# A decode attention kernel: TensorE's code walked twice, and the wait for the stores in a section of its own

## The chip, the cores and the metric

The kernel runs on one core of a Trainium2 chip. The metric is the device time of one execution in microseconds (us). Three executions of the kernel before took 826.02, 824.43 and 824.61 us; their median is 824.61 us.

## What is computed

Two attention layers, A and B, each for a single new token (batch 1, one query row), with 32 heads of 128 columns, caches of 16384 positions and a model width of 512. B looks at the last 4096 positions alone. The rest is the same for both:

```
q = (x @ wq) split into 32 heads
scores = q . k * 128 ** -0.5          # per head, over the positions
p = softmax(scores)
o = p @ v                             # per head
out = o (32 heads x 128, in a row) @ wo    # 512 columns
result = concatenate(out of A, out of B)   # 1 x 1 x 1024, bf16
```

A reads all of k and v, B a quarter of them. One query row means that each byte of k and v is used once.

## The kernel before, in words

**Units.** The work is cut into 20 units, numbered in the order B0, A0 to A15, B1, B2, B3. A unit of A holds two heads, one of B four heads; either one has 8 MB of k and 8 MB of v. k has two buffers in SBUF, v has one.

**Engines.** SyncE (SP) issues the loads of k, v and the weights. VectorE (DVE) multiplies k by q (L365), adds the products up in a tree (L377, L384) and takes maxima (L393, L416). TensorE (PE) turns the per-lane maxima into a row (L399, `unit_max`), spreads the maxima (L421, `max_all`), sums the exponentials (L472, `soft_sum`), multiplies p by v (L492, `pv`) and picks each head's columns (L514, `columns`). ScalarE (ACT) does the exponentials and the copies. DVE works on the scores of one unit while PE and ACT finish the one before it.

**Stream.** `_Stream` keeps a list of operations for each engine and works out which semaphores each has to wait on. `finish` (L140) writes them out, engine by engine. Operations of the A units are marked as one loop (`st.loop`), and `_emit_loop` (L123) writes the body once, inside a hardware loop (`Fori`, L132). So PE's code is, in this order: the projections and unit B0; the loop that serves A0 to A15; then, written out, B1 and B2, the output projection of A, and B3 with the output projection of B. All of it is passed once, from top to bottom.

**The end.** The last unit, B3, is split up to follow its loads. Its v comes in two halves: VL0 in a k buffer and VL1 in the v buffer (L678). For each half, `pv_columns` (L527) issues 128 matmuls at L532. `permute_o` (L544) then rearranges the heads' results (L548, L549, L553, L560). wo of B is loaded in five pieces of 16, 8, 4, 3 and 1 rows (L601, L683), issued right behind VL1. `project_out_columns` (L575) issues four matmuls for each row, so 64, 32, 16, 12 and 4 at L583, and the first of each piece waits for that piece. DVE adds up (L591), PE transposes (L595), DVE copies to a row (L597), and SP stores it (L598, semaphore outB). The store of A's row (outA) has been issued earlier by ACT (L573). Last, an empty operation on SP waits for both stores (L697).

**The section.** Everything in the stream stands in one critical section (L698). In the built program the section's exit is a round on semaphores: SP signals, every engine answers, SP collects the answers and signals once more. The program's own last barriers (L725) come after it.

Of the kernel before, what the change touches and what calls it, by code (L numbers as in the profile page):

```python
# [12 lines left out]
ACT = mybir.ActivationFunctionType  # L13
# [3 lines left out]
HQ, DH = 32, 128  # L17
# [7 lines left out]
class _Op:  # L25
    def __init__(self, eng, idx, emit, dma, tok, loop):
        self.eng, self.idx, self.emit, self.dma, self.tok, self.loop = eng, idx, emit, dma, tok, loop
        self.known, self.waits, self.takes, self.sem, self.count = None, [], [], None, None


class _Stream:
# [6 lines left out]

    def __init__(self, nc):
        self.nc = nc
        self.eng = {"PE": nc.tensor, "DVE": nc.vector, "ACT": nc.scalar, "SP": nc.sync, "POOL": nc.gpsimd}
        self.ops = {e: [] for e in self.eng}
        self.known = {e: {} for e in self.eng}
        self.writer, self.readers = {}, {}
        self.sems, self.tokens, self.counts, self.taken = {}, {}, {}, set()
        self.loop = {}

    def sem(self, name):  # L50
        if name not in self.sems:
            self.sems[name] = self.nc.alloc_semaphore(name)
        return self.sems[name]

    def _mark(self, op):
# [8 lines left out]
        k, v = self._mark(op)  # L64
        return known.get(k, -1) >= v

    def op(self, eng, emit, r=(), w=(), dma=None, tok=None, takes=()):
        assert all(k in self.writer or "." in k for k in r), r
        known = self.known[eng]
        op = _Op(eng, len(self.ops[eng]), emit, dma, tok, self.loop.get(eng))  # L70
        for t in takes:
            src = self.tokens[t].pop(0)
            self.taken.add(t)
            op.takes.append((t, 16 if src.dma is not None else 1))
            self._learn(known, src)
        need = [(self.writer[k], True) for k in [*r, *w] if k in self.writer]
        need += [(x, False) for k in w for x in self.readers.get(k, [])]
        need = [x for x, hard in need if x.eng != eng or x.dma is not None or (hard and eng != "PE")]

        def can_wait(x):  # L80
            if x.sem in self.taken:
                return False
            if op.loop is not None:
                return x.eng == eng and x.loop == op.loop and x.tok is None
            return x.loop is None or x.tok is not None or x.eng == "PE"

        for src in sorted(need, key=lambda x: (not can_wait(x), x.dma is None, -x.idx)):
            if self._knows(known, src):
                continue
            assert can_wait(src), (eng, op.idx, op.loop, src.eng, src.idx, src.sem, src.loop)  # L90
            op.waits.append((src.sem, src.count))
            self._learn(known, src)
        op.known = dict(known)
        if op.loop is not None and eng != "PE" and dma is None and tok is None:
            op.sem = f"{eng}{op.loop[0]}"
            base = sum(1 for o in self.ops[eng] if o.loop == op.loop and o.sem == op.sem)
            op.count = base + 1
        else:
            op.sem = tok or dma or eng
            self.counts[op.sem] = op.count = self.counts.get(op.sem, 0) + (16 if dma is not None else 1)  # L100
        self.tokens.setdefault(op.sem, []).append(op)
        self.ops[eng].append(op)
        for k in r:
            self.readers.setdefault(k, []).append(op)
        for k in w:
            self.writer[k], self.readers[k] = op, []
        return op
# [29 lines left out]
                name, n = own[0].sem, own[-1].count  # L137
                self.eng[eng].wait_ge(self.sem(name), n).then_inc(self.sem(name), -n)

    def finish(self):  # L140
        for eng in ("SP", "ACT", "POOL", "DVE", "PE"):
            ops, i = self.ops[eng], 0
            while i < len(ops):
                if ops[i].loop is None:
                    self._emit(eng, ops[i])
                    i += 1
                    continue
                j = i
                while j < len(ops) and ops[j].loop is not None and ops[j].loop[0] == ops[i].loop[0]:
                    j += 1  # L150
                self._emit_loop(eng, ops[i:j])
                i = j


@with_exitstack
def kernel(
# [14 lines left out]
    nc = tc.nc  # L171
# [46 lines left out]
    A, B = _Side(), _Side()  # L218
# [11 lines left out]

    NA, NB = HQ // 2, HQ // 8
    NT = NA + NB
    st = _Stream(nc)
    V, T_, S, G, L = nc.vector, nc.tensor, nc.scalar, nc.gpsimd, nc.sync

    def by_head(s, ap):
# [247 lines left out]
    def pv(un):  # L484
        s, n, g = un.s, un.n // 4, un.s.groups

        def mms():
            for i in range(n):
                for v in range(s.parts):
                    r0 = 32 * (v * g + i % g)  # L490
                    l = v * n + i
                    x = T_.matmul(  # L492
                        s.o[r0 : r0 + un.rows, :],
                        lhsT=un.pm[:, l, :, :].rearrange("p a b -> p (a b)"),
                        rhs=VS[:, 4 * l : 4 * l + 4, :],
                        start=(i < g), stop=(i >= n - g),
                    )
            return x

        st.op("PE", mms, r=["v0", "v1"] + [f"pm0.{j}" for j in range(4)], w=["o" + s.n], takes=["V0"] if s is A else ["V0", "V1"], tok="pv")  # L500

    def evict(un):
        s = un.s
# [23 lines left out]
    def pv_columns(un, v, V_t, vk, ps, pk, pmk, takes):  # L527
        s = un.s

        def mms():  # L530
            for l in range(un.n):
                x = T_.matmul(  # L532
                    ps[:, 0 : s.nh], lhsT=V_t[:, l, :], rhs=un.pm[:, (v * un.n + l) // 4, :, l % 4],
                    start=(l == 0), stop=(l == un.n - 1),
                )
            return x

        st.op("PE", mms, r=[vk] + [f"{pmk}.{j}" for j in range(4)], w=[pk], takes=takes)
        st.op("DVE", lambda: V.tensor_tensor(  # L539
            out=s.O[:, un.col(v) : un.col(v) + s.nh], in0=ps[:, 0 : s.nh],  # L540
            in1=r_t[:, v * s.nh : (v + 1) * s.nh], op=ALU.mult,
        ), r=[pk, "r"], w=[f"O{s.n}.{un.col(v)}"])
# [19 lines left out]
    def project_out_rows(s, key):  # L562
        ps = oc_t[0:1, 0:DN]

        def mms():
            for r in range(HQ):
                x = T_.matmul(ps, lhsT=s.Op[:, r : r + 1], rhs=s.wo_t[:, r, :], start=(r == 0), stop=(r == HQ - 1))
            return x

        st.op("PE", mms, r=["Op" + s.n, key], w=["oc"])  # L570
        row = osb[0:1, 0 : DN // 2].bitcast(BF16)
        st.op("ACT", lambda: S.copy(row, ps), r=["oc"], w=["osb"])
        st.op("ACT", lambda: S.dma_start(out=out[0, 0:1, 0:DN], in_=row), r=["osb"], w=["outA"], dma="outA")  # L573

    def project_out_columns(s, key, pieces):  # L575
        nf, npc = DN // P, len(pieces)
        ps = OC2[:, 0 : npc * nf].rearrange("p (k c) -> p k c", k=npc)
        r0 = 0
        for k, n in enumerate(pieces):
            def mms(k=k, n=n, r0=r0):  # L580
                for c in range(nf):
                    for r in range(r0, r0 + n):
                        x = T_.matmul(  # L583
                            ps[:, k, c : c + 1], lhsT=s.wo_t[:, r, c * P : (c + 1) * P], rhs=s.Op[:, r : r + 1],
                            start=(r == r0), stop=(r == r0 + n - 1),
                        )
                return x

            st.op("PE", mms, r=["Op" + s.n, f"{key}.{k}"], w=["oc2"])
            r0 += n  # L590
        st.op("DVE", lambda: V.tensor_reduce(  # L591
            out=cols[:, :], in_=ps.rearrange("p k c -> p c k"), axis=AX.X, op=ALU.add
        ), r=["oc2"], w=["cols"])
        pr = TP[0][0:nf, 0:P]
        st.op("PE", lambda: T_.transpose(pr, cols[:, :], identf[:, :]), r=["cols", "identf"], w=["tp0"])  # L595
        rows = p_t[0:nf, 0:P]
        st.op("DVE", lambda: V.tensor_copy(rows, pr), r=["tp0"], w=["p.0", "p.1"])  # L597
        st.op("SP", lambda: L.dma_start(out=out[0, 0, DN : 2 * DN].rearrange("(c f) -> c f", c=nf), in_=rows),  # L598
              r=["p.0"], w=["outB"], dma="outB")
# [4 lines left out]
    for s in (B, A):  # L604
        s.x_row = flat(KS[1][0:1, :, :])[:, x0 : x0 + D]
        for a, b in ((0, D // 4), (D // 4, D // 2), (D // 2, D)):
            st.op("ACT", lambda s=s, a=a, b=b: S.dma_start(out=s.x_row[:, a:b], in_=s.x[0, 0:1, a:b]),
                  w=["x" + s.n], dma=f"x{s.n}{a}")
# [15 lines left out]
    for s in (B, A):  # L624
# [9 lines left out]
          w=["k10", "k11", "xA", "xB"] + [f"k10.{j}" for j in range(4)], dma="K10")  # L634
# [59 lines left out]
    pv_columns(un, 1, VS[:, 0:CH, :], "v0", OC2, "oc2", "pm1", ["pm1"])  # L694
    permute_o(B)
    project_out_columns(B, "wo", wo_pieces)
    st.op("SP", lambda: None, r=["outA", "outB"], w=["end"])  # L697
    with tc.tile_critical(no_gpsimd_drain=True):  # L698
        st.finish()


# [28 lines left out]
```

## Time and profile before

| | |
|---|---|
| median of three executions | 824.61 us |
| the profiled execution's own time | 825.75 us |
| its span in the profile | 823.9 us |
| VectorE busy | 762.6 us (93%) |
| TensorE matmuls busy | 197.0 us (24%), 1985 matmuls |
| ScalarE busy | 60.0 us (7%) |
| moved by DMA | 352.45 MB, 428 GB/s over the span |

The span runs from the first to the last recorded instruction; 1.85 us of the profiled execution's own time lie outside it. All moments below are microseconds from the start of the span. An entry such as "PE oc L583 x112" is a group of 112 instructions of TensorE of line 583 that write the tile oc. The view of the DMA queues counts a queue of kind "instruction" apart from the data queues: what engines load of their own code. Code before the loop, the loop and the code behind it are told apart by the unit that they serve.

### The profile page before, as it was taken

To read this page: it belongs to the slowest core of one execution; us is meant where nothing else is said; L and a number is where in the kernel's file an instruction comes from. 1 tells how busy PE (TensorE), PEld (TensorE's weight loads), DVE (VectorE), ACT (ScalarE), POOL (GpSimd) and SP (SyncE) were. 2 spreads that over 40 slices of the span, in tenths; PEclk is the share of its full clock that TensorE was granted. 3 is DMA by queue.
4 is the path that set the end of the run, shared out by engine and by line. 5 is a ranking of instruction groups with operands and counts; after the bars stand their busy time and mean duration, and the time that the engine had idled before them with its cause. 6 is when DMAs were issued, how large, how long until landed. Compare 5 with 4: busy or idle time off the path is not lost. (4 is left out here: it accounts for less than half of the span.)

```text
span 823.9 us, 5048 instructions
## 1 busy us (share of the span) xinstructions
PE 197.0 (24%) x1985; PEld 98.7 (12%) x1985; DVE 762.6 (93%) x353; ACT 60.0 (7%) x168; POOL 0.7 (0%) x6
## 2 busy tenths in 40 slices
PE   0710313213030403030312213030303030213265
PEld 0200101101010101010101101010101010101125
DVE  2399999999999999999999999999999999999980
ACT  0100100001010101010000000010101000010110
POOL 0000000000000000000000000000000000000000
PEclk9965555555565556565556565565655565655585
DMA  9999999999999999999999999999999999999996
GB/s 382 433 433 433 456 411 449 417 449 420 449 423 442 433 433 436 430 439 426 445 420 449 420 452 414 452 417 449 417 449 417 449 412 433 433 433 432 433 429 268
DMA packets 8095, 352.45 MB, mean 428 GB/s; under 512 B 915, under 2 KB 1046, under 8 KB 1302
## 3 DMA queue, kind: packets, MB, share of 16 engines
q1 hardware_dynamic: 8072, 352.33, 99.1%
q8 instruction: 6, 0.10, 0.0%
q14 instruction: 3, 0.02, 0.0%
q10 hardware_dynamic: 14, 0.00, 0.0%
HBM read 352.32 MB, written 0.00 MB: 428 GB/s over the span
## 5 line engine op out<-in xcount | busy, mean ns | idle before, releaser
L377 DVE TENSOR_TENSOR k<-k 128x8192 bf16<-128x8192 bf16 (+3 forms) x160 | 344.9, 2156 | 4.8
L365 DVE TENSOR_TENSOR k<-k,qA 128x16384 bf16<-128x16384 bf16 x32 | 277.9, 8684 | 1.7 <-DVEq L116 1.7
L492 PE MATMUL oA<-v,pm 128*8 128x512 bf16 x1024 | 91.2, 534 | 28.5 <-PEq L116 28.5
L399 PE MATMUL sm<-identf,m 128*1 128x128 f32 x24 | 8.1, 370 | 322.6 <-PEq L116 322.6
L365 DVE TENSOR_TENSOR k<-k,qB 128x16384 bf16<-128x16384 bf16 x8 | 69.5, 8684 | 6.6 <-ACT qB L354 6.6
L421 PE MATMUL sm<-one_f,Mr 1*128 1x1 f32 x48 | 12.3, 335 | 168.4 <-PEq L116 168.4
L384 DVE TENSOR_REDUCE sc<-k 128x128 f32<-128x1024 bf16 x40 | 48.8, 1220 | 0.7
L399 PEld LDWEIGHTS sm<-identf,m 128*1 128x1 f32 x24 | 1.7, 80 | 324.6 <-issue 324.6
L440 ACT ACTIVATE bias<-sm 128x1 f32<-128x1 f32 (+1 forms) x20 | 3.4, 171 | 506.4 <-ACTq L116 506.4
L492 PEld LDWEIGHTS oA<-v,pm 128*8 128x8 bf16 x1024 | 30.4, 112 | 82.3 <-issue 74.6
L421 PEld LDWEIGHTS sm<-one_f,Mr 1*128 1x128 f32 x48 | 11.2, 299 | 174.8 <-issue 174.8
L504 ACT ACTIVATE osb<-oA,r 128x512 f32<-128x512 f32 x16 | 11.0, 687 | 133.5 <-ACTq L116 133.5
L514 PE MATMUL oc<-selA,osb 128*128 128x2 f32 x128 | 16.4, 250 | 16.2 <-PEq L116 16.2
L492 PE MATMUL oB<-v,pm 128*16 128x512 bf16 x192 | 17.5, 545 | 8.3 <-PEq L116 8.3
L514 PEld LDWEIGHTS oc<-selA,osb 128*128 128x128 f32 x128 | 15.5, 191 | 23.8 <-issue 23.8
L472 PE MATMUL sm<-cs,rowsA 128*128 128x1 f32 x32 | 8.9, 348 | 32.2 <-PEq L116 32.2
L430 ACT ACTIVATE pm<-p,maskA 128x256 bf16<-128x256 bf16 x32 | 14.5, 500 | 0.5
L472 PEld LDWEIGHTS sm<-cs,rowsA 128*128 128x128 f32 x32 | 8.0, 310 | 33.1 <-issue 33.1
L393 DVE TENSOR_REDUCE m<-sc 128x1 f32<-128x256 f32 (+1 forms) x20 | 8.4, 420 | 3.2 <-DVE sc L384 0.5
L444 ACT ACTIVATE p<-sc,bias 128x256 bf16<-128x256 f32 (+1 forms) x24 | 11.3, 470 | 0.6
L347 PE MATMUL tp<-v,k 128*128 128x512 bf16 x32 | 9.7, 479 | 0.3 <-DVE xTA L327 0.3
L327 DVE CAST xTA<-tp 128x4 bf16<-128x4 f32 x1 | 0.2, 162 | 10.2 <-PE tp L320 10.2
(73 smaller groups left out, 110.6 us busy)
## 6 DMA issues: line engine op xcount, KB each, us to landing
k<-in_B_k_cache_dram SPq DMA_DIRECT2D x8, 4096.0 KB, 31.8
v<-in_B_v_cache_dram SPq DMA_DIRECT2D x7, 4096.0 KB, 29.7
v<-in_B_wq_dram SPq DMA_DIRECT2D x1, 4096.0 KB, 12.3
v<-in_A_wq_dram SPq DMA_DIRECT2D x1, 4096.0 KB, 30.6
k<-in_A_wo_dram SPq DMA_DIRECT2D x1, 4096.0 KB, 28.8
k<-in_B_v_cache_dram SPq DMA_DIRECT2D x1, 4096.0 KB, 38.1
v<-in_B_wo_dram SPq DMA_DIRECT2D x1, 2048.0 KB, 25.9
v<-in_B_wo_dram SPq DMA_DIRECT2D x1, 1024.0 KB, 27.8
```

Of the source, the lines that this page charges most:

```text
L347: x = T_.matmul(out_ap, lhsT=s.xb[:, j, c, :], rhs=wq[:, c, j, g : g + 4, :], start=(k == 0), stop=(k == n - 1),)
L365: return V.tensor_tensor(out=k, in0=k, in1=s.q[:, bass.ds(i, 1), :].broadcast_to([P, CH, DH]), op=ALU.mult)
L377: st.op("DVE", lambda it=None, w=w: V.tensor_tensor(out=k[:, :, 0:w], in0=k[:, :, 0:w], in1=k[:, :, w : 2 * w], op=ALU.add), r=[kk], w=[kk])
L384: st.op("DVE", lambda it=None: V.tensor_reduce(out=sc[:, u * CH : (u + 1) * CH], in_=k[:, :, 0:8], axis=AX.X, op=ALU.add), r=[f"k{un.k}{u} ...
L399: i = T_.transpose(sm[0:1, v * P : (v + 1) * P], m_t[:, v : v + 1], identf[:, :])
L421: i = T_.matmul(sm[:, 256 + v : 257 + v], lhsT=Mr[:, v * P : (v + 1) * P], rhs=one_f[:, :], start=True, stop=True,)
L430: return S.activation(out=out, in_=in_, func=ACT.Copy, scale=mask)
L444: st.op("ACT", lambda it=None, v=v: S.activation(out=p_t[:, v * n : (v + 1) * n], in_=sc[:, v * n : (v + 1) * n], func=ACT.Exp, scale=inv, ...
L472: i = T_.matmul(sm[v * w : (v + 1) * w, 264:265], lhsT=s.rows[:, :, :, :].rearrange("p r a b -> p (r a b)"), rhs=cs[:, v : v + 1], start=T ...
L492: x = T_.matmul(s.o[r0 : r0 + un.rows, :], lhsT=un.pm[:, l, :, :].rearrange("p a b -> p (a b)"), rhs=VS[:, 4 * l : 4 * l + 4, :], start=(i ...
L504: st.op("ACT", lambda it=None: S.activation(out=osb[:, :], in_=s.o[:, :], func=ACT.Copy, scale=r_t[:, 0:1]), r=["o" + s.n, "r"], w=["osb"] ...
L514: x = T_.matmul(oc_t[:, 0:w], lhsT=osb[:, j * P : (j + 1) * P], rhs=sel[:, j, :], start=(j == 0), stop=(j == 3),)
```

## The change

PE's operations up to the first one in the loop are written out as before. All the rest, from the loop to the end, is put into a hardware loop of two turns (`Fori(0, 2)`). Inside, the code is cut into seven sections, each behind a branch on the turn's number: in turn 0 each branch skips its section, in turn 1 none does. A section is closed once the sizes of its operations reach 50 matmuls (`size`; the A loop counts as its first operation, 2). In the built program the sections hold: the A loop and B1 up to its L492; B1's L514 and B2 up to L492; B2's L514, A's output projection and B3 up to the first 128 matmuls of L532; the second 128 of L532; `permute_o` and the first 64 matmuls of L583; the next 60; the last 4 with the transpose of L595. Each section adds one compare-and-branch to PE's stream, the outer loop its counter and its own branch. The streams of the other engines are the same up to their ends.

The empty SP operation behind the stores is gone. Instead a second critical section, which names SP alone as its engine, follows the first; in it SP waits for outA and outB. In the built program SP passes the exit of the first section without having waited for the stores, then waits in the second, then passes that one's exit, in which no other engine takes part. The semaphores now come from the tile context's allocator.

```diff
-    def __init__(self, nc):
-        self.nc = nc
+    def __init__(self, tc):
+        self.tc, self.nc = tc, tc.nc
...
-            self.sems[name] = self.nc.alloc_semaphore(name)
+            self.sems[name] = self.tc.alloc_semaphore(name)
...
+    def _runs(self, ops):
+        i = 0
+        while i < len(ops):
+            j = i + 1
+            if ops[i].loop is not None:
                 while j < len(ops) and ops[j].loop is not None and ops[j].loop[0] == ops[i].loop[0]:
                     j += 1
-                self._emit_loop(eng, ops[i:j])
-                i = j
+            yield ops[i:j]
+            i = j
...
+    def finish(self):
+        for eng in ("SP", "ACT", "POOL", "DVE"):
+            for run in self._runs(self.ops[eng]):
+                self._emit_run(eng, run)
+        runs = list(self._runs(self.ops["PE"]))
+        n = next(i for i, run in enumerate(runs) if run[0].loop is not None)
+        for run in runs[:n]:
+            self._emit_run("PE", run)
+        pe = self.nc.tensor
+        with pe.Fori(0, 2) as second:
+            i = n
+            while i < len(runs):
+                with pe.If(second):
+                    size = 0
+                    while i < len(runs) and size < 50:
+                        self._emit_run("PE", runs[i])
+                        size += sum(o.size for o in runs[i][:1])
+                        i += 1
...
-    st.op("SP", lambda: None, r=["outA", "outB"], w=["end"])
     with tc.tile_critical(no_gpsimd_drain=True):
         st.finish()
+    with tc.tile_critical(sync_engine=mybir.EngineType.SP, no_gpsimd_drain=True):
+        for name in ("outA", "outB"):
+            nc.sync.wait_ge(st.sem(name), 16)
```

## The prediction

> **What bounds the kernel now.** I read the page's slices first.
>
> ```profile
> DMA  9999999999999999999999999999999999999996
> q8 instruction: 6, 0.10, 0.0%
> ```
>
> The DMA engines are full from the first slice to the last but one, so up to about 803 us the transfers set the pace, and what another engine loses there costs nothing while its slack lasts. The second line (queues: packets, MB) says that one queue loaded code: six packets, 0.10 MB, so some 16 KB each. Next the chain that ended last, in order of time (start, length, what).
>
> ```profile
> 787.43 21.56 DMA v<-in_B_v_cache_dram
> ...
> 809.04 0.72 PE oc L532 x21
> 809.76 1.25 issue
> 811.01 3.01 PE oc L532 x107
> ...
> 814.26 0.30 PE tp L548
> ...
> 814.95 0.30 PE tp L553 x4
> ...
> 815.60 0.57 PE oc L583 x16
> 816.17 1.07 issue
> 817.24 3.16 PE oc L583 x112
> 820.40 0.02 issue
> 820.43 0.19 DVE cols L591
> ```
>
> VL1 lands at 809.00, and from there TensorE is the path. Twice it stops in the middle of a row of equal matmuls, for 1.25 and 1.07 us, waiting for nothing that the profile knows. Between the stops lie 107 + 1 + 4 + 16 = 128 matmuls with a weight load each: 256 instructions, and 16 KB / 256 = 64 bytes for one. So I take it that code comes in pages of 256 instructions and that TensorE stood at their edges. The DMA view cut into narrow windows bears that out. Queue 8's packets start at 90.1, 128.6, 783.3, 808.4, 814.6 and 818.3 us. Counting back from the stops by 256 instructions, the edges fall into the matmuls of L492 of B0 (85.8 on), of the loop's first turn (122.8 on) and of B2 (779.6 on), and into the first half of L532 (about 805). Each packet starts some 3.5 us behind such an edge: entering a page calls for the next. In the tail: edge passed at 811.01, packet at 814.6, about 1.06 us long (3.3% of sixteen engines over 2 us in the window 808 to 810, and much the same here), TensorE again at 817.24. That is **6.2 us from call to use** beside full DMA queues, while 256 instructions of the tail take 128 x 27.5 ns = 3.5 us. Code is late there, and only there does it cost time.
>
> **The tail after the change.** If turn 0 brings all pages in and they stay, both stops go. L532 would end at 814.02 - 1.25 = 812.77 and L583 begin at 815.60 - 1.25 = 814.35. What is late next is wo of B. Its pieces in the DMA view (KB, us from issue to landing; issued at 788.02, 788.65, 789.13, 789.60 and 790.1):
>
> ```profile
> v<-in_B_wo_dram SPq DMA_DIRECT2D x1, 2048.0 KB, 25.9
> v<-in_B_wo_dram SPq DMA_DIRECT2D x1, 1024.0 KB, 27.8
> v<-in_B_wo_dram SPq DMA_DIRECT2D x1, 512.0 KB, 28.5
> v<-in_B_wo_dram SPq DMA_DIRECT2D x1, 384.0 KB, 29.0
> v<-in_B_wo_dram SPq DMA_DIRECT2D x1, 128.0 KB, 28.8
> ```
>
> They land at 813.9, 816.45, 817.6, 818.6 and 818.9. Walk L583 against that at 27.5 ns a matmul. 64 matmuls: 814.35 to 816.1. The 32 wait for 816.45: to 817.35. The 16 wait for 817.6: to 818.05. The 12 wait for 818.6 and a wake of 0.04 (VL1 landed at 809.00, L532 began at 809.04): to 818.97. The last 4: 0.11, and 0.14 until the last leaves the array (one takes 165 ns): 819.22. Before, L583 ended at 820.40. So the tail wins **1.18 us, not 2.32**: the second stop is mostly replaced by a wait for the weights.
>
> Branches: seven in turn 1, of which those ahead of 809 and the one behind L532 lie under waits (814.02 to 814.26 is a wait for VectorE), and the one after 64 matmuls ends before the 816.45 landing. One is left on the path, ahead of the last 4. No view shows a branch of TensorE by itself. Lower bound 0: matmuls already issued cover it. Upper bound from VectorE's loop, whose idle time per turn (1.7 us over 6, page and waits) is 0.28 us for a counter, a taken branch and a semaphore. I take 0.08, nearer 0, as this branch is not taken and turns no counter.
>
> **The end.** The store is issued at 821.38 for 0.35 us; SP's row of waits gives 0.8 us until it lands, at 822.5; the span ends at 823.9. Now the first section's exit runs during the store's flight, but a second wait and a second exit follow it. In the built program, SP's instructions between the store's wait and the last barriers are seven before and six after; the other engines are no longer asked. Bounds: 0 (as much added as removed) to -0.8 us (all that fits under the flight comes off). I take -0.2, near the count of instructions. Sum: -1.18 + 0.08 - 0.2 = **-1.3 us**.
>
> **Turn 0, the cost that must be hidden.** The loop starts behind B0's last matmul. Rows of TensorE's and VectorE's timelines:
>
> ```profile
> 92.69 1.03 PE L514 MATMUL oc<-selB,osb 128*128 128x8 f32 x8 [0.97 <-PEq L116]
> 110.75 0.37 PE L399 MATMUL sm<-identf,m 128*1 128x128 f32 x1 [17.03 <-PEq L116]
> ```
>
> ```profile
> 119.12 0.27 DVE L416 TENSOR_REDUCE M<-sm 1x2 f32<-1x128 f32 x1
> ```
>
> TensorE has 17.0 us free; its result of 110.75 is first read at 119.12. Counted in instructions, the loop's head lies in the page that B0's L492 enters; the sections end in the second to the sixth page from the start, so turn 0 touches every page. The second is there (packet 90.1); the third to the sixth have to come, each called when the branch reaches the page ahead of it: 4 x 6.2 = 24.8 us, and some 0.2 us for each of seven branches by VectorE's row: 93.7 + 24.8 + 1.4 = 119.9. L399 takes 0.4, so VectorE would wait 1.2 us at L416, once. That comes out of the loads' lead: the next v load hangs on this unit and is issued at 131.41, when the load before it (issued 109.73, 30.8 us to landing) has 9.1 us left. So 119.1 + 9.1 - 0.4 = 127.8 is the point up to which turn 0 costs **nothing**; it has some 8 us to spare, a little less where single DMA engines finish earlier. If that cover is gone, each microsecond costs one. The number of code packets stays at six, so the DMA engines carry the same bytes.
>
> [...]
>
> **Rivals.**
> 1. *Pages do not stay.* If the memory holds few pages, turn 0 pushes the loop's own out again; they come back while TensorE has slack (one more 6.2 us for the head: 126.1, still under 127.8), and the tail stops as before. Left are the end and one branch: -0.2 to +0.5 us, 824.5. For it: no row shows more than a few pages held. Against it: the loop straddles an edge (57 of 64 matmuls into L492), the page behind it was loaded at 128.6, and queue 8 has no packet from 130 to 750; so at least three pages stay through fifteen turns.
> 2. *Turn 0 is too long*, the one on the slower side. If a branch into a page that is still on its way calls for it again behind the first call, a page costs 2 x 6.2: 4 x 12.4 = 49.6, ending at 144.7, which is 17 us past 127.8. The DMA engines then stand for those 17 us, minus the 1.3: about 840. It decides from 8.5 us a page on. Against it: the six loads seen took about 6.2 where both ends can be read; for it: none of those was called by a branch.
> 3. *The whole 2.3 us*, if the pieces of wo land earlier relative to TensorE than in this execution, and half of the end's bound: 822.0. Against it: in the window 818 to 819 us the DMA engines still move 28 GB/s.
>
> **How the numbers follow.** The profiled execution's own time is 825.75, its span 823.9, so I expect a span near 822.6 and 824.45 for such an execution. The median of the runs is 1.14 lower: 824.61 - 1.3 = 823.3. A measurement can tell about 0.2%, 1.65 us, from no change. Chances: forecast 0.60, its own range 822.1 (end at -0.8, landings 0.5 earlier) to 824.1 (branch 0.28, end 0, landings 0.5 later); rival 1 0.12; rival 2 0.14; rival 3 0.14. Of the forecast's 2.0 us some two fifths lie beyond 1.65 us of gain (under 822.96): faster 0.24 + 0.14 = 0.38; within 0.2%: 0.36 + 0.12 = 0.48; slower 0.14. The range takes in the forecast, rivals 1 and 3: 822.0 to 825.2.
>
> **What would show it.** Right: five or six packets of queue 8 between 90 and 125 us and none later; the chain without "issue" inside L532 and L583, and in their place L583 waiting for v<-in_B_wo; L399 of A0 at 118 to 120; L416 of A0 held up by a microsecond; 0.1 to 0.3 us less between the store's landing and the end. Wrong: packets of queue 8 in the tail (rival 1); a dip in the DMA slices near 140 us and L399 of A0 behind 128 (rival 2); L583 unbroken and ended before 818.9 (rival 3).

## The result and the profile after

The changed kernel takes **827.88 us** (median of 7 runs, 827.65 to 828.17), the kernel before 824.77 (7 runs, 824.43 to 826.02). The ratio is 1.0034, with 95% between 1.0024 and 1.0044: slower by 3.1 us, where 1.3 us of gain were forecast, and outside the forecast range of 822.0 to 825.2. The profiled execution's own time is 827.88 and its span 826.1, so again some 1.8 us lie outside the span.

The units' code stands 26 lines lower in the changed file: L399, L416, L421, L532, L583 and L598 of before are L425, L442, L447, L558, L609 and L624. (In e9 it stands one line lower than in before, in e5 one lower than in the change.)

The page of the changed kernel has the same first two lines as before, but for the last digit:

```profile
DMA  9999999999999999999999999999999999999995
q8 instruction: 6, 0.10, 0.0%
```

Again six packets of code. Their moments are what changed: 90.2, 97.2, 104.8, 111.9, 119.1 and 126.4 us in narrow windows of the DMA view, and from 127 to the end that view lists no queue 8. The chain that ended last (start, length, what):

```profile
809.71 0.04 issue
809.76 6.98 PE oc L558 x256
816.74 0.02 issue
...
818.32 3.57 PE oc L609 x128
821.89 0.02 issue
```

Both stops are gone: 256 matmuls in one piece, then 128 in one piece. But the chain no longer begins at the load of VL1. Before, the first 128 of these matmuls ran from 804.63, while VL1 was on its way. Now they begin at 809.76, 0.7 us after VL1's landing (issued at 787.4, 21.7 us to landing: 809.1, before 809.0), and the 128 that need VL1 queue behind them. Where does it come from? TensorE's timeline at turn 0:

```profile
92.59 1.03 PE L540 MATMUL oc<-selB,osb 128*128 128x8 f32 x8 [0.98 <-PEq L121]
123.06 0.37 PE L425 MATMUL sm<-identf,m 128*1 128x128 f32 x1 [29.44 <-PEq L121]
```

and VectorE's beside it:

```profile
110.45 8.68 DVE L391 TENSOR_TENSOR k<-k,qA 128x16384 bf16<-128x16384 bf16 x1
123.58 0.28 DVE L442 TENSOR_REDUCE M<-sm 1x2 f32<-1x128 f32 x1 [4.45 <-DVEq L121]
123.89 0.21 DVE L443 COPY Mr<-M 1x128 f32<-1x128 f32 x1
...
133.93 8.68 DVE L391 TENSOR_TENSOR k<-k,qA 128x16384 bf16<-128x16384 bf16 x1
```

Turn 0 kept TensorE's first result of A0 back until 123.4, where it came at 111.1 before. VectorE, done with A1's first product at 119.13 (it works one unit ahead of the maxima), stood for 4.45 us ahead of A0's maxima. In VectorE's list of waits (us in total, times, longest) it is this row:

```profile
DVE M L442 <- DVEq L121: 5.3, 2, 4.4
```

In before it is 0.7 us, once, at the end; the second of the two here is that one, 0.9. Now cut each trace into the stretch from A0's maxima to the start of B3's last product. Before (stretch, its length, then busy us and count of PE, PEld, DVE, ACT, POOL, and clock, DMA share, GB/s):

```profile
119.20:780.40 661.20, 142.41 (x1331) 69.11 (x1335) 651.66 (x282) 46.77 (x132) 0.00 (x0) 0.57 1.00 432
```

and after:

```profile
123.50:784.90 661.40, 145.35 (x1387) 69.90 (x1387) 651.78 (x281) 46.79 (x132) 0.00 (x0) 0.57 1.00 433
```

Two things are full here, not one. The DMA engines are at 1.00, and VectorE is busy for 651.7 of 661.2 us, 98.6%; what is left lies in gaps between its instructions, of which its list of waits names six in either trace, 1.7 us in all and 0.3 us the longest. Measured from instruction to instruction, the stretch takes 661.23 us before and 661.29 after. VectorE never makes up what it lost.

### The profile page after: what moved, and what is told of

It is laid out like the page before. It is cut to its first block, busy times and chain, and to the rows that moved or that the text cites. A ratio compares the mean times of both kernels' runs of the same rounds, so it can differ in the third digit from the quotient of the medians.

```text
span 826.1 us, 5076 instructions
## 1 busy us (share of the span) xinstructions
PE 195.7 (24%) x1985; PEld 98.1 (12%) x1985; DVE 762.8 (92%) x353; ACT 60.0 (7%) x168; POOL 0.7 (0%) x6
## 5 line engine op out<-in xcount | busy, mean ns | idle before, releaser
L425 PE MATMUL sm<-identf,m 128*1 128x128 f32 x24 | 8.3, 379 | 371.3 <-PEq L121 371.3
L447 PE MATMUL sm<-one_f,Mr 1*128 1x1 f32 x48 | 12.8, 344 | 160.6 <-PEq L121 160.6
L425 PEld LDWEIGHTS sm<-identf,m 128*1 128x1 f32 x24 | 1.7, 80 | 373.3 <-issue 373.3
L447 PEld LDWEIGHTS sm<-one_f,Mr 1*128 1x128 f32 x48 | 11.6, 310 | 167.1 <-issue 167.1
L442 DVE TENSOR_REDUCE M<-sm 1x2 f32<-1x128 f32 (+1 forms) x20 | 6.0, 299 | 5.3 <-DVEq L121 5.3
```

The lines of the kernel that those rows point to most:

```text
L425: i = T_.transpose(sm[0:1, v * P : (v + 1) * P], m_t[:, v : v + 1], identf[:, :])
L447: i = T_.matmul(sm[:, 256 + v : 257 + v], lhsT=Mr[:, v * P : (v + 1) * P], rhs=one_f[:, :], start=True, stop=True,)
```

## The experiments

Two theories stood at first. **T1**: VectorE runs without a pause from A0's maxima to its last product, so its 4.45 us come out at the far end, and TensorE's last matmuls start that much later. **T2**: the loads' lead covers the wait, as the prediction had it; the loss comes from the new end and the branches.

All before-kernels quoted here ran on the same chip as the kernel beside them. "The walk" is turn 0's pass over TensorE's branches. The profiles are collected in one table first; moments in us, "lost" is VectorE's wait or added work between A1's first product and A0's maxima.

| kernel | A1's first product starts | lost | A0's maxima | B3's first 128 matmuls start | last output matmul ends | own time |
|---|---|---|---|---|---|---|
| before | 110.52 | 0 | 119.12 | 804.63 | 820.40 | 825.75 |
| the change | 110.45 | 4.45 | 123.58 | 809.76 | 821.89 | 827.88 |
| e1, the walk alone | 108.82 | 6.00 | 123.50 | 809.66 | 821.78 | 827.09 |
| e3, walk from B0 on | 109.64 | 0 | 118.24 | 804.43 | 819.60 | 825.03 |
| e8, as e3 | 109.30 | 0 | 117.90 | 804.57 | 819.41 | 824.72 |
| e12, as e3, 5 memsets | 109.18 | 3.2 | 121.03 | 806.94 | 819.19 | 824.54 |
| e13, as e3, 9 memsets | 111.74 | 5.8 | 126.26 | 812.38 | 824.50 | 829.78 |
| e4, before, 9 memsets | 108.08 | 5.8 | 122.59 | 808.71 | 822.97 | 828.45 |
| e6, before, 3 memsets | 110.88 | 1.8 | 121.40 | 807.49 | 822.16 | 827.62 |
| e9, before, second section | 107.01 | 0 | 115.61 | 803.16 | 819.12 | 824.80 |

From A0's maxima to B3's first matmuls it is 685.5 to 686.7 us in every row but the last.

### e1, e11, e14: the walk without the new end

```diff
-            self.sems[name] = self.tc.alloc_semaphore(name)
+            self.sems[name] = self.nc.alloc_semaphore(name)
...
+    st.op("SP", lambda: None, r=["outA", "outB"], w=["end"])
     with tc.tile_critical(no_gpsimd_drain=True):
         st.finish()
-    with tc.tile_critical(sync_engine=mybir.EngineType.SP, no_gpsimd_drain=True):
-        for name in ("outA", "outB"):
-            nc.sync.wait_ge(st.sem(name), 16)
```

> The two turns over TensorE's code as in the change, but the end of before: one section, the empty SyncE operation that waits for both stores. Theory T1 (turn 0 takes 29.5 us, holds VectorE up by 4.5 us at the maxima of A0, and VectorE, which has no pause from there to the end, never makes that up; the new end adds some 0.7 us by itself): span about 825.4 us, time about 827.2 us, VectorE's wait of 4.4 us at L442 still there, both stops of TensorE in the tail gone. Rival T2 (what costs is the new end together with the branches, VectorE's wait being covered by the lead of the loads): time 824 to 825.3 us.

Measured: 825.94 us (10 runs, 824.41 to 829.93) against 824.81; ratio 1.0007 [0.9991, 1.0023]. The median says little here, because the runs fall in two groups: five from 824.4 to 824.9, four from 826.9 to 827.1, one of 829.9. The profiled execution is of the second group (827.09). In it VectorE waits 6.00 us at A0's maxima, the maxima come at 123.50, and the tail is that of the change.

> e1_walk_only once more, unaltered, on another occasion: a second look at whether its times fall in two groups, near 824.6 and near 827.0 us. If the profiled execution is one of the upper group: VectorE's wait at L442 is 4 to 6 us and turn 0 ends at about 123 us; if it is one of the lower: the wait is under 2 us and turn 0 ends before 121 us.

The same kernel on another chip: 827.04 (12 runs), ratio 1.0014 [1.0002, 1.0026], again five at 824.6 to 825.2, six at 827.0 to 827.7 and one of 829.6. The profile is of the second group: 5.85 us of wait, maxima at 123.45.

> e1_walk_only, for its profile: whether the first code packet comes at 87.5 us (seen in three kernels' profiles) or at 90.0 us (in all profiles of the change and of e1_walk_only). At 87.5 us, turn 0 would end some 2.5 us earlier, A0's maxima come at about 121 us, and the time belongs to the group near 824.7 us; at 90.0 us, 123.5 us and 827.0 us.

825.9 (8 runs; four at 824.7 to 824.8, three at 827.0 to 827.3, one of 829.7), ratio 1.0010 [0.9994, 1.0026]. The profile fell in the second group once more: 5.23 us of wait, maxima at 123.39. So no execution of the first group was profiled here either.

### e7: the change once more

> The change itself, unaltered, on the chip of these runs. Five of ten runs of e1_walk_only took 824.4 to 824.9 us and four took 827 us. If VectorE's start decides (early enough in some executions to absorb the wait), the change shows the same two groups, 0.7 to 0.9 us higher: about 825.3 and 827.9 us. If it is always late: all runs at 827.6 to 828.2 us.

No edit, on another occasion than the seven runs of the result. 827.73 us (12 runs) against 824.90, ratio 1.0023 [1.0010, 1.0035]: five at 825.3 to 825.5, six at 827.6 to 828.1, one of 830.2. The profile (827.96) shows 5.72 us of wait. So the change too has the two groups, each some 0.5 to 1 us above e1's; the seven runs of the result were all in its upper one.

### e2, e9, e10: the new end without the walk

e2 is before with the end of the change: the second section on SP and the semaphores from the tile context.

> The kernel before with the new end alone: the second section in which SyncE waits for both stores, and semaphores from the tile context; TensorE's code is passed once, as before. From the profiles of the change and of e1_walk_only (2.0 against 1.35 us between the store's landing and the end): the new end costs 0.7 us, so the span is 0.6 to 0.8 us and the time 0.5 to 0.9 us above before. If instead it costs nothing by itself and the slower end was a result of TensorE's two turns: within 0.2 us of before.

825.74 us (11 runs) against 824.90, ratio 1.0015 [1.0006, 1.0023]: slower by 0.8 us, with both stops still there (0.79 and 1.07 us). From the issue of the store to the end of the span it is 3.2 us (821.18 to 824.4), as in the change (822.87 to 826.1), where before has 2.5 (821.38 to 823.9). SP's waits before and in the change show how (us in total, times, longest):

```profile
SPq L118 <- DMA out_dram<-p: 0.8, 1, 0.8
SPq L725 <- PEq L725: 0.5, 2, 0.4
```

```profile
SPq L753 <- PEq L753: 0.8, 2, 0.7
SPq L742 <- PEq L742: 0.7, 1, 0.7
SPq L753 <- DMA out_dram<-p: 0.2, 1, 0.2
```

The exit of the first section (L742) does run under the store's flight: the wait for the store is 0.2 us instead of 0.8. But something behind it takes longer than the exit saved. Two runs took it apart.

> The kernel before with the second section of SyncE, but semaphores allocated as before. The new end of e2_end_only took 2.0 us from the store's landing to the end, against 1.33 in before. If the section costs it: 1.6 to 2.0 us again here, time 0.3 to 0.9 us above before. If the allocator costs it, which clears its semaphores at the close: 1.3 us or a little less here, time within 0.2 us of before.

Only the second section (the hunk at the end; semaphores as before): 825.17 (10 runs), ratio 1.0004 [0.9995, 1.0013], 2.9 us from the store's issue to the end.

> The kernel before with the tie of its semaphores to the tile context alone; one section and the empty SyncE operation as before. If the allocator costs the new end: 1.9 to 2.1 us from the store's landing to the end, time 0.5 to 0.9 us above before. If the section does: 1.3 us, the time of before.

Only the allocator (`self.tc.alloc_semaphore(name)`), with the old end: 825.02 (10 runs), ratio 0.9999 [0.9990, 1.0008], 2.8 us. So the section gives about 0.4 and the allocator 0.3 of the 0.7 us in the span (all eleven profiles with the old end and allocator have 2.5). Neither can be told from nothing by its median; only both together can (e2).

e9's profile shows one more thing. It passes its code once, as before does, yet the first stop is not in it:

```profile
803.16 3.55 PE L533 MATMUL oc<-pm,k 128*128 128x4 bf16 x128 [0.60 <-PEq L117]
809.04 3.58 PE L533 MATMUL oc<-pm,v 128*128 128x4 bf16 x128 [2.34 <-DMA v<-in_B_v_cache_dram]
...
815.54 2.72 PE L584 MATMUL oc<-OpB,v 128*128 128x1 bf16 x96 [0.75 <-issue]
818.53 0.59 PE L584 MATMUL oc<-OpB,v 128*128 128x1 bf16 x16 [0.28 <-DMA v<-in_B_wo_dram]
```

VectorE came to A1's first product 3.5 us earlier here (107.01), so the first 128 matmuls ran earlier, crossed into the new page earlier, and the next page was there in time (its packet starts at 806.9, where before's starts at 808.4); the second stop is 0.75, and behind it TensorE already waits for wo. That is a tail with nearly nothing left for the walk to win.

### e3, e8: the walk where TensorE has time

The walk of e1 (old end, old allocator), begun eight operations into PE's list, ahead of unit B0, where TensorE waits for VectorE anyway (28.3 us in before).

```diff
-        n = next(i for i, run in enumerate(runs) if run[0].loop is not None)
+        n = 8
```

> As e1_walk_only, but the loop of two turns begins before unit B0's first operation of TensorE, when TensorE has been free since 43.6 us and is next needed at 72.0 us, and its result at about 80.5 us. T1: turn 0 takes five pages of 7.1 us and ends at about 80 us, so VectorE waits 0 to 1 us; then the tail is bound by the landings of B's wo as predicted, and the time is 823.2 to 824.6 us. T2 (branches or the outer loop cost in the tail, not the delay): as e1_walk_only, no more than 0.3 us apart.

824.57 us (11 runs, 824.34 to 825.03) against 824.81, ratio 0.9993 [0.9984, 1.0002].

> e3_walk_early once more, unaltered: turn 0 ahead of B0's operations, the end of before. T1: VectorE is not held up at A0; both stops of the tail gone, waits for wo in L583 in their place; 0.2 to 1.2 us under before. If e3's gain was chance: the same as before or slower.

Once more, on another chip: 824.72 (11 runs, 824.62 to 824.84) against 824.90, ratio 0.9997 [0.9988, 1.0005]. No second group either time. The profile of e8 has six packets of code from 44.0 to 76.9 us, no wait of VectorE at the maxima of B0 or A0, and this tail of TensorE:

```profile
809.23 3.57 PE L558 MATMUL oc<-pm,v 128*128 128x4 bf16 x128 [1.10 <-DMA v<-in_B_v_cache_dram]
...
814.40 1.85 PE L609 MATMUL oc<-OpB,v 128*128 128x1 bf16 x64 [0.37 <-ACT OpB L586]
816.61 1.01 PE L609 MATMUL oc<-OpB,v 128*128 128x1 bf16 x32 [0.37 <-DMA v<-in_B_wo_dram]
817.87 0.58 PE L609 MATMUL oc<-OpB,v 128*128 128x1 bf16 x16 [0.24 <-DMA v<-in_B_wo_dram]
818.82 0.59 PE L609 MATMUL oc<-OpB,v 128*128 128x1 bf16 x16 [0.37 <-DMA v<-in_B_wo_dram]
```

It is the tail that the prediction worked out: VL1, no stop, then wo piece by piece, ending at 819.41 (e3: 819.60), where 819.22 was forecast and before had 820.40. And yet the medians move by 0.2 us, within the interval. The walk's gain is real against the profiled execution of before, and almost nothing against its median.

### e4, e6: VectorE's loss alone

Before, with memsets of a PSUM tile on VectorE between A1's first product and A0's maxima. They compute nothing that is used (the tile is overwritten later).

```diff
         scores_prod(un, 0)
+        if T == 2:
+            for _ in range(9):
+                st.op("DVE", lambda: V.memset(OC2[:, :], 0.0), w=["oc2"])
```

> The kernel before, with nine memsets of a PSUM tile that is not in use put into VectorE's order ahead of the maxima of A0, some 4.5 us of VectorE time, once, at about 119 us. No change to TensorE's code. T1 (VectorE cannot make up lost time): everything VectorE does to the end is 4.5 us later; the first 128 matmuls of B3's v start at 809.1 to 809.7 instead of 804.6 us, and the time rises by 3 to 4.5 us, to about 828.5 us. T2 (lost time of VectorE comes out of the lead of the loads): 824.5 to 825.2 us.

829.44 us (5 runs, 827.97 to 831.83) against 824.81, ratio 1.0057 [1.0038, 1.0075]. Each memset took 0.67 us with its gap, so the loss was 5.8 and not the 4.5 that was meant.

> As e4_dve_delay, with three memsets instead of nine: about 2.0 us of VectorE, once. T1 (VectorE never makes it up, and ends 0.9 to 3 us ahead of need, by how early it starts): the first 128 matmuls of L532 end up to 2.0 us later than before, and the time rises by 0 to 1.3 us. If lost time were made up on the way: the chain's L393 of B3 no more than 0.3 us later against the start of VectorE's A0 than in before, and no change in time.

Three memsets, 1.8 us: 826.05 (11 runs) against 824.90, ratio 1.0013 [1.0004, 1.0022]. In TensorE's tail of e6 the matmuls of B3 start at 807.49 and the stop inside them has grown:

```profile
807.49 3.56 PE L532 MATMUL oc<-pm,k 128*128 128x4 bf16 x128 [0.60 <-PEq L116]
810.90 0.70 PE L532 MATMUL oc<-pm,v 128*128 128x4 bf16 x21
814.00 2.99 PE L532 MATMUL oc<-pm,v 128*128 128x4 bf16 x107 [2.40 <-issue]
```

1.8 us of VectorE's time, lost 680 us before the end and with the DMA engines full (9 in 39 of the 40 slices of e4's page), cost 1.2 us; 5.8 us cost 4.6. T1 stands, and T2 falls, but for the 0.7 us of the end.

### e12, e13: from which point it costs

The memsets again, now on top of e3, where the code is in place and the tail has no stops.

> e3_walk_early (code brought in before B0, so no stops in the tail) with five memsets, some 3.3 us of VectorE time, ahead of A0's maxima, which then come at about 121.3 us instead of 118.0. From there to B3's last product VectorE needs 661.25 us in every profile so far, so the first L558 starts at about 807.4 us; the second half is ready at 811.0 instead of 809.2, and L609 reaches its last piece at about 819.5, level with the landing of wo. T1 with a knee there: 824.6 to 825.4 us. If any lateness of VectorE shows in full: 827.5 us or more.

Five memsets, 3.2 us, maxima at 121.03: 824.85 us (10 runs) against 825.04, ratio 0.9998 [0.9987, 1.0008]. Nothing is lost. The two lines of its tail that say why:

```profile
810.35 3.55 PE L558 MATMUL oc<-pm,v 128*128 128x4 bf16 x128
...
815.50 3.69 PE L609 MATMUL oc<-OpB,v 128*128 128x1 bf16 x128 [0.37 <-ACT OpB L586]
```

The second half follows the first without waiting for VL1, and L609 runs in one piece and ends at 819.19, level with the last landing of wo (818.9): the waits for loads have been used up to the last tenth.

> The same with nine memsets, 6.0 us: A0's maxima at about 124.0 us, the first L558 at about 810.1 us, 256 matmuls in one row, the end 2.5 to 3 us behind e3_walk_early: 827.0 to 827.7 us, about what the slower executions of e1_walk_only take (827.0), whose maxima come at 123.5 us. If what costs in e1_walk_only were not VectorE's lateness: under 826 us.

Nine memsets, 5.8 us: 827.98 (10 runs, 826.04 to 829.78), ratio 1.0029 [1.0017, 1.0040]. The profiled execution, the slowest of the ten, had also come to A1's first product late (111.74); its maxima come at 126.26, L609 ends at 824.50.

So the knee, the point up to which VectorE's lateness is free, is at **A0's maxima at 121 us**. The rows give the same point by themselves: L609 begins 8.56 us behind B3's first matmuls when nothing waits (815.50 - 806.94; in the change 818.32 - 809.76) and takes 3.56, so it ends 12.1 behind them; to be level with wo's 818.9 they must start by 806.8, and A0's maxima lie 686 us ahead of that: 120.8. Behind the knee the cost is about one for one: against e12 the maxima are 2.55 us later in the change and 5.23 in e13, and the last output matmul ends 2.70 and 5.31 us later.

### e5: jumping over the middle of the code

e1 with a first section that reaches to the first half of B3's v, so that turn 0 jumps over the middle of the code instead of touching each page.

```diff
-            i = n
+            i, least = n, 200
...
-                    while i < len(runs) and size < 50:
+                    while i < len(runs) and size < least:
...
                         i += 1
+                least = 50
```

> As e1_walk_only, but the first section reaches from the A loop to the first 128 matmuls of B3's v, so turn 0 jumps over the middle of the code and touches the last three pages alone. T1: three pages of 7.1 us end turn 0 at about 116 us, before VectorE asks for A0's maxima at 119.1 us; VectorE waits less than 0.3 us, both stops of the tail go, L583's matmuls then wait for B's wo: time 823.2 to 824.0 us, 1.0 to 1.4 us under before. T2: no more than 0.3 us apart from e1_walk_only. If pages do not outlive the jump: stops in the tail and the time of before.

825.65 us (11 runs, 825.40 to 825.99) against 824.81, ratio 1.0003 [0.9994, 1.0012]. Turn 0 is shorter, and VectorE doesn't wait (maxima at 116.72). But the page lists ten packets of code, and the last four come at 783.4, 806.9, 813.2 and 818.2 us, as in before: what turn 0 had loaded was loaded again. A stop is back:

```profile
q8 instruction: 10, 0.16, 0.1%
```

```profile
814.17 0.49 PE L610 MATMUL oc<-OpB,v 128*128 128x1 bf16 x13 [0.37 <-ACT OpB L587]
815.82 1.50 PE L610 MATMUL oc<-OpB,v 128*128 128x1 bf16 x51 [1.16 <-issue]
```

## Why the prediction was wrong, point by point

- **Pages, stops and what a stop waits for: right.** One of the six packets came ahead of the walk, four during it, the last 3 us behind it, and none in the tail; both rows of matmuls are unbroken. Rival 1, by which pages do not stay, fell for a walk that touches each page in order, and holds for one that jumps over the middle (e5: ten packets). After its six packets, fifteen turns of the loop and the tail of the change ran without another (none from 127 us on); how much code TensorE holds no run shows.
- **"So the tail wins 1.18 us": right where it can be seen.** e8 against the profiled execution of before: 820.40 - 819.41 = 0.99 (e3: 0.80). In the change it is covered by the later start.
- **"8.5 us a page", "6.2 us from call to use": the size was off.** In turn 0 the packets lie 7.0 to 7.6 us apart, so the first result came at 123.06 + 0.37 and not at 119.9 + 0.4. That is still under 8.5 a page, so by the prediction's own rule it should have cost nothing. The 6.2 had been read in the tail. In the walk of e8 both rates can be seen: 7.2 to 7.4 us between the packets at 44.0, 51.4 and 58.6, then 5.9 to 6.4 to those at 64.6, 70.5 and 76.9. In the first stretch queue 1 moves 6.36 MB in 97 packets (66 KB each), in the second 7.67 MB in 256 (30 KB). In the change from 90 to 120 us they are 58 KB, in before's tail from 811 to 817 us 4.5 KB. The longer intervals go with the larger packets, but not in proportion (6.2 us goes with 30 KB and with 4.5 KB); that one causes the other was not tried.
- **"That comes out of the loads' lead ... So 119.1 + 9.1 - 0.4 = 127.8 is the point up to which turn 0 costs nothing": this is the step that failed.** The lead was there, and the DMA engines never stood still for want of it: VL1 landed at 809.1 instead of 809.0, and A's loads of k took 29.3 us (median) from issue to landing where they had 32.9, so the lead shrank and held. But the lead only keeps the loads on time. VectorE is a second chain beside them, 98.6% busy from A0's maxima to B3's last product, and it too ends in TensorE's tail. The slices of before, of which the prediction read the row of the DMA engines alone, had it (busy tenths of VectorE):

```profile
DVE  2399999999999999999999999999999999999980
```

The point from which it counts is where B3's first matmuls no longer end ahead of the loads: 121 us, not 127.8. The true 123.6 lies between. Had a page cost 6.2 us, the maxima would have been at 120.3, just on the cheap side, and the mistake would not have been seen.
- **The end, "I take -0.2": wrong sign.** The exit of the first section was hidden as said (0.6 us less of a wait), but the second section and the other allocator of semaphores add more: +0.7 us. The count of instructions did not tell their price.
- **"The median of the runs is 1.14 lower: 824.61 - 1.3": wrong in method.** The difference between the profiled execution and the median was treated as a constant. But the loss to be removed is itself part of what differs between executions: with TensorE's code passed once, the two stops add up to 2.32 us in the profile of before, 1.86 in e2, 1.79 in e10 and 0.75 in e9. No execution at the median was profiled, so how much of the 1.14 us it was stays open. e3 and e8 show what the walk is worth on the median: -0.2 us, not told from nothing.
- **Rival 2 had the right place and the wrong mechanism.** It wanted the DMA engines to stand from 127.8 on and 840 us. They never stood; the price was 2.5 us, behind a knee at 121.
- **Branches, 0.08:** no cost is seen. L609's 128 matmuls take 3.57 us with two branches between them, and L583's 3.56 without any in e4.

The account closes with measured terms. L609 ends at 821.89 instead of 819.41 (e8, whose runs have their median at its profile's own time, 824.72): +2.48. The end adds 0.7. 824.72 + 2.48 + 0.7 = 827.9, against 827.88. From the profiled execution of before it is 825.75 + 1.49 + 0.7 = 827.9 as well. How the start of the tail moved by 5.13 us for 4.46 of VectorE's lateness can be read too: TensorE's small steps ahead of it were slower (L447 0.98 us where L421 had 0.57; L425 0.59 where L399 had 0.38), after 5.65 us without work instead of 1.29 (4.51 us later at the start of L425, then 0.21 and 0.41 more).

**What stays open** is why e1 and the change fall in two groups. The lower one lies where the kernel before lies (e1) or 0.5 us above (e7), as if VectorE's wait had stayed under the knee. The traces narrow it down. In the twelve that run B0 ahead of any walk, the first packet of code comes at one of two moments: near 87.5 us where B0's `pv` matmuls began at 82.2 to 83.4 us (e4, e5, e9), near 90.0 where they began at 84.1 to 86.1 (the other nine). So in these traces the packet moves in steps, not with TensorE. All five profiles of e1 and the change have it near 90.0, and A0's maxima at 123.4 to 123.6, though their matmuls began up to 1.6 us apart. One step earlier, the maxima would come at about 121 us, on the knee. The groups, too, lie 2.4 to 2.6 us apart, and the single times of 829.6 to 830.2 lie 2.3 to 2.9 above the upper one. An estimate of the step: at the 433 GB/s of the slices, sixteen engines take 2.4 us over one data packet of 66 KB each (34 packets, 2.23 MB, from 85 to 90 us in the change), so it may be one such packet ahead of the code. But no execution of the lower group was profiled, so this is argued, not shown. Nor is every late execution the walk's: of the 117 runs of before beside the experiments, nine took 827 us or more.

## What to carry to other kernels

Full DMA engines did not make VectorE's time free here (5.8 us of it cost 4.6 in e4): before giving an engine a wait, cut the trace from there to the end and see whether it ever pauses. VectorE, 98.6% busy, did not, and its wait came out at the end, less only what its last result had stood waiting there (3.2 us cost nothing in e12). A gain read from a profiled execution is to be taken from that execution's time, and the median asked separately whether it has the same loss. Work that fills a gap of one engine (here loading code ahead) goes where that engine's next result is not yet wanted: begun ahead of B0 the same walk cost nothing (ratios 0.9993 in e3 and 0.9997 in e8).

## What the runs showed of the hardware

- TensorE's code came in 16 KB packets (queue 8: six, 0.10 MB, in before and in the change). On a walk by branches one came each 7.0 to 7.6 us beside data packets of 58 to 66 KB (the change, e8), each 5.9 to 6.4 us beside 30 KB ones (e8). The prediction had one price for both.
- The first packet came near 87.5 us in three traces and near 90.0 in nine, and nowhere between, while the start of the matmuls ahead of it ranged over 3.9 us.
- After a walk through the code in order no packet of code came for 700 us (the change, six in all); after a walk that jumped over the middle four more came, from 783.4 to 818.2 us (e5, ten in all).
- Four matmuls of one column took 0.98 us where TensorE had been idle for 5.65 us one step ahead of them (L447 in the change), and after 2.00 us (e12), but 0.57 us where it had been idle for 1.29 (L421 in before).
- A second critical section for SP and semaphores from the tile context's allocator added 0.4 and 0.3 us to the span, behind the last store (e9, e10).
